# Unread products at the start of a sparse-attention and MLP kernel: eighty-eight in 64 columns for forty-four in 128, and one fewer ahead of the third local score round

## The chip, the cores and the metric

The kernel runs on one core of a Trainium2 chip. A core has five engines that run their own instruction streams side by side: TensorE (PE in the profile, with its weight loads listed as PEld), VectorE (DVE), ScalarE (ACT), GpSimd (POOL) and SyncE (SP). They wait for each other through semaphores, and transfers run on 16 DMA engines. The metric is the device time of one execution in microseconds (us); lower is better.

## The reference

Attention with fixed sparse masks on 8 batches, 8 heads, 576 positions and 64 channels, and then a two-layer MLP over the 4608 tokens (512 to 2048 to 512) with the Mish activation:

```python
scores = scale * np.matmul(q, k.transpose(0, 1, 3, 2))
mask_local = (rel >= 0) & (rel < stride)                       # heads 0 to 3
mask_strided = (rel >= 0) & (pos[None, :] % stride == pos[:, None] % stride)   # heads 4 to 7
attn = softmax(where(mask, scores, -1e9));  x = attn @ v
h = x @ w_in
g = h * np.tanh(sp)          # sp = log(1 + exp(h))
out = g @ w_out
```

`stride` is 32. The inputs and the output are float32; the kernel multiplies in bfloat16.

## The kernel before

The work is cut into 9 MLP blocks of 512 tokens (`NBLK`), and the attention of the next batch is woven in between the products of the current block. Only the places that the masks leave are computed: the local heads in windows of 96 queries against 128 keys, the strided heads in tiles of 72 positions.

The order of each engine's instructions is the order in which the code writes them (`tc.manual_schedule()`): nothing reorders it. What is told here is the beginning, batch 0, which has no MLP to hide behind; it stands in the main body from line 636 on:

- Loads are issued on three queues. `k` for the strided heads goes first on SP and ACT (L645), everything else on POOL: rest of `k` (L646), `q` and `v` of the strided heads (L110), local `k` and `q` (L123), local `v` (L137), the MLP weights `w_in` in five pieces (L166), then batch 1 and `w_out`.
- VectorE clears buffers (L651 to L674), the first of them the 640 columns of `kTs[1]` that the unread products multiply, and casts the first `k` tile (L675).
- TensorE then runs: the unread products (L678); transposes of strided `k` (`t_step`, L237), each copied out of PSUM by VectorE or ScalarE; the mask of each strided part added as a product with the identity (`bias`, L297); three more unread products (L682); transposes of strided `q`; bias; one unread product (L686); bias; three strided score rounds (`qk`, L324), with the exponential on ScalarE (L338); two unread products (L690); then `pv2` for strided tiles in pairs (L366, L371; normalised by VectorE at L396 and L397), in between transposes of the local `k` and `q` (`t_step_loc0`, L253), bias and scores of the local parts 0 and 1; transposes of the strided result (`xt`, L420); two unread products (L709); bias and scores of local part 2; `pv2` of the local windows; and the first MLP groups (`mlp1`, L575).

An unread product is made by `fill`: the cleared part of `kTs[1]` as weights, `w` columns of it as the moving operand, into a PSUM tile that nothing reads. `fill_acc(i, n, w)` takes the accumulator `i` for it; the next user of the same accumulator waits until these products have ended. In the stream each product is two instructions, a weight load (LDWEIGHTS) and a matmul.

The batch's local scores have ten products of 96 columns in parts 0 and 1 and four in part 2. `mlp1(0, accs)` runs its groups 0 and 1 first for the channels of the strided heads (2, 3), between the transposes of the local result, then the other channels, then groups 2 to 7. The whole of what lies between L678 and L717 feeds PE in order, so a product that waits holds up those behind it.

Of the kernel before, what the change touches and what calls it, by code (L numbers as in the profile page):

```python
# [40 lines left out]
def kernel(ctx, tc, q, k, v, moe_w_in, moe_w_out, out):  # L41
# [48 lines left out]
    def acc(i, name):  # L90

        return ps_a.tile([128, 2, 512], F32, tag=f"acc{i}", name=name)
# [451 lines left out]
    def fill(t, n, w=512):  # L544

        for _ in range(n):
            nc.tensor.matmul(
                t[:, 0:w], lhsT=kTs[1][:, 512:640], rhs=kTs[1][:, 0:w], start=True, stop=True
            )

    def fill_acc(i, n, w=512):
        fill(acc(i, "fill")[:, 0, :], n, w)
# [83 lines left out]
    with tc.manual_schedule():  # L636
# [38 lines left out]
        cast(Dv, ks[0][0:PN, 0:2, :], k32[0:PN])  # L675

        a = Attn(0)
        fill_acc(2, 44, 128)  # L678
        for hp in range(2):
            t_step(0, "k", hp, Sc if hp else Dv)  # L680
        a.bias("s", 0, 0)
# [24 lines left out]
        load_w_out(3, 4)  # L706
        a.xt("s", 0, Dv)
        a.xt("s", 1)
        fill_acc(0, 2)  # L709
        a.bias("l", 2, 0)  # L710
        a.qk([("l", 2)], 0)
        Sc.preload_act_table(AF.Mish)
# [119 lines left out]
```

## Time and profile before

| what | us |
|---|---|
| median of 5 runs (lowest, highest) | 309.44 (308.17, 310.79) |
| the profiled execution | 311.34 |
| its span, first to last instruction | 309.6 |
| PE busy (share of the span) | 301.0 (97%) |
| PE, unread products (52 matmuls), first and last start | 1.3 and 20.2 |
| first product of the MLP (L575) starts | 23.3 |
| ACT, POOL, DVE busy | 181.6, 105.4, 157.6 |

The profile is of one execution. Its page gives the busy time of each engine, the span in slices with the clock that TensorE was granted (1.00 is full speed), the DMA queues with their packets, and the chain of work that ended last. Other views list the instructions in order of time, the idle time of an engine before an instruction with what released it in brackets ("issue" is time in which the profile shows nothing that was waited for), and busy times by window. An `xN` at the end of a row counts instructions. Weight loads and products overlap, and the ends of products are modelled.

### The profile page before, as it was taken

Reading aid. Unit: us, or ns where it says so; the run is one execution under the profiler, and the core shown is the slowest. Engines: PE = TensorE matmul, PEld = TensorE weight load, DVE = VectorE, ACT = ScalarE, POOL = GpSimd, SP = SyncE. Lnnn points to the kernel's source line nnn. Section 1 sums busy time; section 2 is a strip of 40 time slices with the busy share of each in tenths; the row PEclk is TensorE's granted clock in tenths of the full one; section 3 lists DMA queues with packets and bytes.
Section 4 is the critical chain, followed back from the end, with each engine's and each line's share of the span. In section 5 each row is a group of like instructions: output and inputs, shape, how many; then the busy total and the mean of one; then the engine's idle time right before and its main releaser. Section 6 shows DMA issues by size and latency. Waiting matters only on the chain.

```text
span 309.6 us, 6027 instructions
## 1 busy us (share of the span) xinstructions
PE 301.0 (97%) x2504; PEld 160.9 (52%) x2504; DVE 157.6 (51%) x375; ACT 181.6 (59%) x193; POOL 105.4 (34%) x119
## 2 busy tenths in 40 slices
PE   8889999999999999999999999999999999999995
PEld 7555545544454445444569654545454544444444
DVE  4346156600870057569686978697869760000000
ACT  2655553577537663767766776677667836215501
POOL 8752339930570052514570089016800000000000
PEclk9959999999999999999999999999999999999999
DMA  8999999999999999999457998898430030011011
GB/s 137 166 205 198 200 174 149 138 162 257 170 161 173 194 162 198 185 210 192 55 88 146 208 178 171 167 190 143 109 103 2 8 126 4 0 68 70 0 66 70
DMA packets 97550, 41.81 MB, mean 135 GB/s; under 512 B 79604, under 2 KB 91460, under 8 KB 97524
## 3 DMA queue, kind: packets, MB, share of 16 engines
q1 hardware_dynamic: 71708, 28.84, 50.4%
q0 software_dynamic: 25504, 12.31, 33.2%
q8 instruction: 19, 0.31, 0.5%
q10 hardware_dynamic: 312, 0.28, 0.3%
q14 instruction: 7, 0.06, 0.1%
HBM read 36.82 MB, written 9.44 MB: 149 GB/s over the span
## 4 chain that ended last, share of the span: by engine, by line
PE 90%; DVE 4%; DMA 2%; issue 1%; POOL 1%; ACT 1%; ACTq 0%; POOLq 0%
PE psh L575 40%; PE pso L599 34%; PE po L366 5%; PE pso L626 4%; PE ps L324 3%; DMA lq<-in_k_dram 2%; DVE x_l L383 1%; DVE x_s L383 1%; PE trx L410 1%; PE trx L420 1%; DVE rden L382 1%; PE tr L253 1%; PE ps L297 1%; DVE Pl L346 1%; ACT Ps L338 0%
## 5 line engine op out<-in xcount | busy, mean ns | idle before, releaser
L575 PE MATMUL psh<-xT,w_in 128*128 128x512 bf16 (+3 forms) x648 | 130.6, 355 | 0.5 <-ACT Ps L338 0.3
L599 PE MATMUL pso<-w_out,gT 128*128 128x512 bf16 x512 | 121.7, 379 | 0.0
L581 ACT ACTIVATE gT<-psh 128x1024 bf16<-128x1024 f32 x72 | 72.4, 1023 | 46.1 <-PE psh L575 46.1
L575 PEld LDWEIGHTS <-w_in 128*128 128x128 bf16 x648 | 60.8, 98 | 55.1 <-issue 0.9
L599 PEld LDWEIGHTS <-gT 128*128 128x128 bf16 x512 | 45.5, 98 | 46.1
L445 DVE STREAM_TRANSPOSE xs_t<-x_s 32x512 bf16<-32x512 bf16 x48 | 33.7, 702 | 0.9
L606 ACT COPY osb<-pso 128x1024 f32<-128x1024 f32 x16 | 17.6, 1102 | 24.8 <-PE pso L599 14.4
L181 POOL CAST kl<-kl 96x768 bf16<-96x768 f32 x10 | 8.8, 908 | 66.8 <-DMA kl<-in_k_dram 66.8
L382 DVE RECIPROCAL rden<-po 72x4 f32<-72x4 f32 (+1 forms) x98 | 17.3, 177 | 28.0 <-PE po L366 27.8
L346 DVE TENSOR_TENSOR Ps<-Ps,consts_sb 72x864 bf16<-72x864 bf16 (+3 forms) x12 | 8.7, 721 | 39.1 <-ACT Ps L338 39.0
L436 DVE STREAM_TRANSPOSE xT<-x_l 32x384 bf16<-32x384 bf16 x48 | 27.3, 569 | 0.7
L181 DVE COPY osb<-pso 128x512 f32<-128x512 f32 (+1 forms) x2 | 1.1, 558 | 51.3 <-PE pso L626 51.3
L383 DVE TENSOR_TENSOR x_s<-po,rden 72x256 bf16<-72x256 f32 x56 | 23.6, 421 | 1.9
L338 ACT ACTIVATE Ps<-ps 72x864 bf16<-72x864 f32 (+3 forms) x21 | 17.4, 860 | 11.3 <-PE ps L324 11.3
L366 PEld LDWEIGHTS <-Ps 72*128 72x128 bf16 x256 | 15.9, 98 | 12.2 <-DVE Ps L346 1.3
L452 ACT COPY xT<-xs_t 128x576 bf16<-128x576 bf16 x8 | 21.4, 2941 | 0.0
L338 ACT ACTIVATE Pl<-ps 128x960 bf16<-128x960 f32 (+1 forms) x20 | 17.3, 876 | 6.2 <-PE ps L324 6.2
L366 PE MATMUL po<-vs,Ps 72*128 72x65 bf16 (+1 forms) x256 | 18.5, 194 | 0.4 <-DVE Ps L346 0.2
L181 POOL CAST vl<-vl 128x768 bf16<-128x768 f32 (+2 forms) x20 | 16.6, 828 | 5.7 <-DMA vl<-in_v_dram 4.4
L383 DVE TENSOR_TENSOR x_l<-po,rden 96x256 bf16<-96x256 f32 x42 | 17.7, 421 | 1.4
L179 ACT COPY xT<-trx 128x576 bf16<-128x576 bf16 x15 | 9.6, 639 | 13.6 <-PE trx L420 9.6
L346 POOL TENSOR_TENSOR Ps<-Ps,consts_sb 72x1008 bf16<-72x1008 bf16 (+1 forms) x9 | 14.5, 1637 | 6.6 <-DVE x_l L383 6.5
(93 smaller groups left out, 245.0 us busy)
## 6 DMA issues: line engine op xcount, KB each, us to landing
out_dram<-osb SPq DMA_DIRECT2D x16, 512.0 KB, 4.8
kl<-in_k_dram SPq DMA_DIRECT2D x5, 576.0 KB, 7.9
ql<-in_q_dram SPq DMA_DIRECT2D x5, 576.0 KB, 10.9
vs<-in_v_dram SPq DMA_DIRECT2D x5, 576.0 KB
vl<-in_v_dram SPq DMA_DIRECT2D x5, 576.0 KB, 10.0
w_out<-in_moe_w_out_dram POOLq DMA_DIRECT2D x4, 512.0 KB, 16.5
ks<-in_k_dram POOLq DMA_DIRECT2D x7, 288.0 KB, 9.0
qs<-in_q_dram POOLq DMA_DIRECT2D x7, 288.0 KB, 9.4
```

Source lines behind the costliest of these rows:

```text
L181: eng.tensor_copy(out_, in_)
L338: nc.scalar.activation(pt[0:n, :, 0:nw], t[0:n, :, o0:o0 + nw], AF.Exp, scale=scale)
L346: meng.tensor_tensor(out=pm, in0=pm, in1=mk[0:n, :].unsqueeze(1).unsqueeze(1).to_broadcast([n, 2, nu, w]), op=ALU.mult,)
L366: nc.tensor.matmul(po[:, h, 0:rhs.shape[-1]], lhsT=pt[0:n, c0:c0 + 128], rhs=rhs, start=True, stop=True,)
L382: nc.vector.reciprocal(rden[0:m, :], po[0:m, :, D])
L383: nc.vector.tensor_tensor(out=dst.rearrange("p (h d) -> p h d", h=4), in0=po[0:m, :, 0:D], in1=rden[0:m, :].unsqueeze(2).to_broadcast([m, ...
L436: nc.vector.transpose(dst[32 * q:32 * q + 32, :, :, m:m + 32], src[m:m + 32, :, :, q, :])
L445: nc.vector.transpose(xs_t[32 * q:32 * q + 32, :, :, m:m + 32], src[m:m + 32, :, :, q, :])
L452: nc.scalar.copy(xT[:, 2 + c, t0:t0 + S].rearrange("p (n j) -> p j n", j=CS), xs_t[:, :, c, 0:PN])
L575: nc.tensor.matmul(ps[:, u, o:o + n], lhsT=w_in[:, cc, fc * 128:(fc + 1) * 128], rhs=xT[:, cc, a:a + n], start=(cc == 2 and o == 0), stop= ...
L581: nc.scalar.activation(gT[:, 2 * g:2 * g + 2, :], ps[:], AF.Mish)
L599: nc.tensor.matmul(p[:, ot % 2, :], lhsT=gT[:, fc, 128 * ot:128 * ot + 128], rhs=w_out[:, fc, :], start=(fc == 0), stop=(fc == 15),)
```

## The change

In line 678 the forty-four unread products of 128 columns become eighty-eight of 64 columns, in the same accumulator and at the same place. In line 709, ahead of the bias and the scores of local part 2, two unread products of 512 columns become one.

```diff
         a = Attn(0)
-        fill_acc(2, 44, 128)
+        fill_acc(2, 88, 64)
         for hp in range(2):
             t_step(0, "k", hp, Sc if hp else Dv)
...
         a.xt("s", 0, Dv)
         a.xt("s", 1)
-        fill_acc(0, 2)
+        fill_acc(0, 1)
         a.bias("l", 2, 0)
         a.qk([("l", 2)], 0)
```

## The prediction

> **What bounds the kernel now.** I read the page first: TensorE (PE) is busy 97% of the 309.6 us span and the chain that ended last lies on it for 90%. So time taken out of PE's stream at the front moves everything behind it, as long as no transfer becomes the limit. Second, the timeline of PE from 9 to 24 us, the stretch that both edits bear on. Its rows give start, length, engine, line, operation and, in brackets, idle time before:
>
> ```profile
> 1.27 4.83 PE L547 MATMUL fill<-kTs 128*128 128x128 bf16 x44 [1.27 <-DVE kTs L651]
> ...
> 14.66 0.26 PE L324 MATMUL ps<-qTl,kTl 64*128 64x96 bf16 x4
> ...
> 16.41 0.42 PE L324 MATMUL ps<-qTl,kTl 64*128 64x96 bf16 x6 [1.49 <-issue]
> ...
> 19.78 1.05 PE L547 MATMUL fill<-kTs 128*128 128x512 bf16 x2
> 20.88 0.48 PE L297 MATMUL ps<-consts_sb 128*128 128x192 bf16 x2
> ...
> 23.30 1.02 PE L575 MATMUL psh<-xT,w_in 128*128 128x512 bf16 x4 [0.23 <-DVE rden L396]
> ```
>
> The first local score round has ten equal products. Four run, PE stops, six follow at 16.41. All ten read operands that the fourth already had; the releaser is "issue", so nothing that the profile shows was awaited. Third, windows over this place (busy us and count of each engine, then granted clock, DMA share, GB/s):
>
> ```profile
> 0.00:14.92 14.92, 12.92 (x222) 10.20 (x223) 5.66 (x25) 7.04 (x10) 11.72 (x20) 1.00 1.21 150
> 12.75:16.16 3.41, 1.91 (x46) 1.44 (x47) 1.78 (x4) 1.58 (x3) 2.72 (x4) 1.00 1.86 166
> 16.16:19.57 3.41, 3.16 (x47) 2.09 (x47) 1.55 (x5) 1.60 (x2) 2.50 (x4) 0.50 1.28 205
> 19.57:22.99 3.42, 3.36 (x39) 2.08 (x36) 1.45 (x3) 2.28 (x4) 0.69 (x1) 0.50 1.25 208
> 23.00:40.00 17.00, 16.77 (x125) 9.19 (x124) 7.11 (x13) 10.41 (x12) 5.87 (x8) 1.00 1.32 198
> ```
>
> The stretch that holds the stop has PE busy for 1.91 of 3.41 us; after it the granted clock is 0.50 for 6.8 us. So the stop costs twice: itself, and half speed behind it. Fourth, the DMA queues: of the whole span, and of 13.5 to 15.2 and 19.9 to 20.9 us (packets, MB, share):
>
> ```profile
> q8 instruction: 19, 0.31, 0.5%
> ...
> q8 instruction: 1, 0.02, 5.9%
> ...
> q8 instruction: 1, 0.02, 5.6%
> ```
>
> Queue q8 brings PE's code: 0.31 MB in 19 packets is 16.3 KB each, for 2504 products and as many weight loads, 264 instructions a packet. One packet moves between 13.5 and 15.2 us, and PE goes on after it. I read the stop as PE having run out of code.
>
> **Where the stop lies in the program.** Before it stand 222 products, 223 weight loads and five waits or branches that the profile doesn't count: 450 instructions. With 256 to a block (16,384 bytes at 64 each), a block begins at 450, the one before at 194. Number 194 lies in the strided score rounds, which begin at 9.44 us after a wait. From entering block 194 to running at 450 is 16.41 - 9.45 = 6.9 us. I take it that entering a block asks for the next one: the second packet, seen from 19.9 us, comes 3.5 us after PE entered block 450 at 16.4, and the first, from 13.5 us, 4.1 after 9.45. A block that PE gets through in under some 6.9 us makes it wait. Block 194 has 256 small instructions; PE did them in 5.3 us (9.45 to 14.72) and waited 1.7.
>
> The Trainium skill speaks against this: "Runtime: NRT & Kernel Launch", section "Instruction fetch mechanics", has blocks of 256 instructions too, but room for 2048 on PE and a boundary cost that is mostly hidden. By it PE would not starve at number 450, the change would save only its one removed product, 0.2 to 0.4 us, and the time would be 309.1. The 19 packets stand against the room (with 2048 held some 12 would do), and the 1.49 us idle row against "hidden". I go by the trace.
>
> **First edit: 88 products of 64 columns for 44 of 128.** *Duration.* They run before the clock is up: 44 in 4.69 us (4.83 with the last one's tail, less about 0.14) is 106.7 ns each, 128 columns at 0.83 ns. At 64 columns that is 53.3 ns, and 88 x 53.3 = 4.69 us: nothing changes. The bound from below is nothing, as the columns are the same. From above: the same skill's "TensorE: Matmul & The Clock Gate", on the gap of 56 ns, has some 62 ns per product where the sequencer decodes in software, so 88 x 62 = 5.46 us, 0.77 late. The row that is nearest denies it: in the same half-speed clock, 16 products of 64 and 1 columns with 16 weight loads start within 0.62 us (16.77 to 17.39), 39 ns each. I take 0; 0.8 is kept for the range. The cover is thin: the first q transposes wait for their load until 7.79, an idle of 0.15 us.
>
> *Position.* Eighty-eight more instructions before everything else. The block at 194 now begins at what was 106, the last of the first eight k transposes, which PE passes at 6.17 us at the latest. Adding 6.9 makes the next block ready by 13.1. That block begins at what was 362, the third pair of the local q transposes. These wait for their load until 12.93, so it is wanted at 12.97: **what is left of the stop is 0.0 to 0.15 us.** The 1.69 us (14.72 to 16.41) go. The next boundary, at 706, was 620 (86 on, since the second edit takes two away): the fourth product of the MLP's first group. Asked for at 13.0, ready at 19.9; wanted, below, at 20.2. Blocks after that take far longer than 6.9 us (the last row above: 249 instructions in 17 us).
>
> **Clock.** Without the stop, the stretch from 12.75 us loses nearly 1.5 us of idle; what waits remain (0.3 for the bias round, 0.3 for the transposes) are like those of 9.33 to 12.75, after which the clock stayed at 1.00. So I carry on at full speed from 14.72. The score round ends at 14.9; 32 products of pv2("s", 6) at 27 ns (10.80, 10.84, 10.87 in the timeline) end at 15.4. VectorE ends the pair before at 15.70 and needs 0.20 + 0.04 + 0.69, so x_s is whole at 16.65. Meanwhile bias and scores of the second local round run from 15.75 to 16.4. Sixteen transposes at 33 ns go from 16.7 to 17.25.
>
> **Second edit: one filler product fewer.** Now two take 19.78 to 20.83, and the bias round behind them waits for their end (20.88). At full speed one product is 0.22 us less on PE; at half speed 0.41. The remaining one ends at 17.65, bias and scores at 18.1 to 18.2, and the first eight of pv2("l", 0) at 18.5. VectorE is free since 18.1 (transpose copy of 0.76 us from 17.3), divides from 18.55 to 19.48, and the MLP's first group starts 0.15 later: 19.6, where it was 23.30. **The sum is -3.7 us:** 1.7 stop, 0.2 filler, 1.8 clock.
>
> **What could hide it.** Transfers now have 3.7 us less time. The five pieces of w_in are issued from 10.2 to 14.0 and take up to 12.4: the last is there at 26.4, and its first reader starts at 30.5 instead of 34.2. The first w_out piece lands at 16.65 + 16.5 = 33.1, wanted at 35.0 (38.66 - 3.7); the k and q pieces of batch 1 (15.66 + 14.8 = 30.5) at 32 to 34; its v piece (17.41 + 17.2 = 34.6) at 35.7. All hold, the closest by 1.1 us. No queue is moved past: neither edit issues a DMA, and POOL's issues wait for other transfers. Later PE is full, so the 3.7 us arrive at the end.
>
> **To the runs.** The profiled execution took 311.34 us for a span of 309.6, the median of the runs is 309.44, from 308.17 to 310.79. On its own scale the change makes 311.34 - 3.7 = 307.6. The five runs may pay the half clock in different measure: the gain in full off the slowest gives 307.1, stop and filler alone (1.9) off the fastest 306.3. Between them: **306.7 us**, 0.9% faster.
>
> **Rivals.** (1) The stop goes but half speed comes anyway, since idle shares near this place are enough for it, or the fillers run 0.8 us longer and the block comes late by as much: 309.44 - 1.7 = 307.7, up to 308.8. For it: the threshold isn't known, 1.91 of 3.41 busy was too little and 3.16 was enough. (2) The change doesn't do what it says, PE's code having nothing to do with the idle time: 309.2. Against it: the stop amid ten equal products. (3) Slower: the code packet moves at 13.5 us because the DMA engines are loaded (share 1.86), not because PE asked at 9.45. Then it is there at 16.4 as before, but PE needs it at 12.97: a stop of 3.4 us, and 1.9 us of products still to do behind it, in part at half clock: 309.44 + 1.7 + 0.9 = 312. It decides from the point at which the code comes later than 14.7. Against it: the second packet came 3.5 us after its block was entered, under the same load.
>
> **Numbers.** Forecast 0.66, rival 1 0.17, rival 2 0.07, rival 3 0.10. The forecast's own range is 305.4 to 307.9; with rival 1 the range is 305.4 to 308.9, which leaves out rivals 2 and 3. A measurement of this kernel tells 0.5% (1.5 us) from no change: below 307.9 lie the forecast and half of rival 1, 0.75; within, its other half and most of rival 2, 0.14; above 311.0 0.11.
>
> **What would show it.** Right: no idle row above 0.3 us inside the first local round, clock 1.00 from 6 to the end, first L575 product at 19.6, a q8 packet at about 10 us. The step on duration: 88 fillers from 1.27 to 5.96. Wrong: an idle row at the local q transposes near 13 us that lasts to 16.4 (rival 3), a 0.50 stretch with no stop ahead of it (rival 1), or the stop again after four of the ten products (rival 2).

## The result and the profile after

The changed kernel takes 307.63 us in the median of 44 executions (306.42 to 312.78), the kernel before 310.79 in the median of 79 (307.22 to 316.57). The ratio is 0.9915, with a 95% interval of 0.9897 to 0.9933; like all ratios below it leaves out executions more than 1.5% above the fastest of their kernel, here all 11 of the changed kernel's in which PE had half clock and only 13 of the 79 of before, while the means over all executions, 308.45 and 310.48, differ by 0.65%. The profiled execution took 307.29 us, with a span of 305.5 (before 311.34 and 309.6).

Rows of TensorE from the timeline of the changed kernel:

```profile
1.27 4.35 PE L547 MATMUL fill<-kTs 128*128 128x64 bf16 x88 [1.27 <-DVE kTs L651]
...
13.47 0.70 PE L253 MATMUL tr<-consts_sb,lq 96*64 96x96 bf16 x24 [0.54 <-DMA lq<-in_q_dram]
...
15.03 0.50 PE L324 MATMUL ps<-qTl,kTl 64*128 64x96 bf16 x10
...
17.48 0.38 PE L547 MATMUL fill<-kTs 128*128 128x512 bf16 x1
17.92 0.32 PE L297 MATMUL ps<-consts_sb 128*128 128x192 bf16 x2
...
19.91 1.02 PE L575 MATMUL psh<-xT,w_in 128*128 128x512 bf16 x4 [0.47 <-DVE rden L396]
```

The ten products of the first local score round now stand in one row: the stop between the fourth and the fifth is gone. The only longer idle rows ahead of them wait for loads. The MLP starts at 19.91 instead of 23.30, 3.4 us earlier; the other 0.7 of the 4.1 us of span come behind that point. The same stretches as in the windows of before (busy us and count by engine, granted clock, DMA share, GB/s):

```profile
12.75:16.16 3.41, 2.81 (x77) 2.19 (x74) 1.81 (x5) 2.39 (x5) 2.24 (x4) 1.00 2.05 159
16.16:19.57 3.41, 3.23 (x59) 2.05 (x59) 2.96 (x7) 2.87 (x5) 3.01 (x4) 1.00 1.28 200
19.57:22.99 3.42, 3.08 (x27) 2.00 (x28) 3.09 (x6) 1.98 (x3) 0.70 (x1) 1.00 1.24 206
```

PE is busy for 2.81 us where it was for 1.91, and the clock stays at 1.00. The code queue, over the span and from 8.3 to 9.5 us:

```profile
q8 instruction: 20, 0.33, 0.5%
...
q8 instruction: 1, 0.02, 4.9%
```

There is one packet more for 86 instructions more, and the first one moves near 8.5 us, where it was after 13.5.

Both kernels come in executions that differ by how long PE had half clock. The mean clock of an execution falls into steps: 1.00, 0.994, 0.989, 0.983, 0.978, which are 0 to 4 stretches of 3.41 us at half clock (3.41 x 0.5 / 308 = 0.0055; half clock lasted 6.8 us, two stretches, in the windows of before). Sorted so, with 147 executions of the kernel before that ran beside the experiments and 64 of the changed one:

| stretches at half clock | before: executions, median us | changed: executions, median us |
|---|---|---|
| none | 26, 308.05 | 52, 307.27 |
| 1 | 40, 310.16 | 0 |
| 2 | 74, 311.31 | 0 |
| 3 or 4 | 7, 312.8 | 12, 311.5 |

Among executions at full clock the change is worth 0.8 us; before, those with one or two stretches of half clock took 2.1 or 3.3 us more than those with none. Before, 121 of 147 executions had half clock; after, 12 of 64 (11 of the first 44, 1 of 20 later). Weighted, the change saves 310.5 - 308.1 = 2.4 us: by these classes a third at full clock (stop and filler) and two thirds from fewer executions with half clock. The split is not a clean one: half speed for 3.41 us can lose 1.7 us of products at most, so the 2.1 hold something else too, perhaps a longer stop.

### The profile page after: what moved, and what is told of

Its sections match the earlier page's. It is cut to its first block, busy times and chain, and to the rows that moved or that the text cites. A ratio compares the mean times of both kernels' runs of the same rounds, so it can differ in the third digit from the quotient of the medians.

```text
span 305.5 us, 6113 instructions
## 1 busy us (share of the span) xinstructions
PE 297.6 (97%) x2547; PEld 159.0 (52%) x2547; DVE 155.8 (51%) x375; ACT 181.6 (59%) x193; POOL 105.7 (35%) x119
## 4 chain that ended last, share of the span: by engine, by line
PE 89%; DVE 3%; DMA 3%; issue 1%; POOL 1%; ACT 1%; ACTq 0%; POOLq 0%
PE psh L575 41%; PE pso L599 33%; PE pso L626 5%; PE po L366 5%; PE ps L324 3%; DMA lq<-in_q_dram 3%; DVE x_l L383 1%; PE trx L410 1%; ACT Ps L338 1%; DVE x_s L383 1%; PE tr L253 1%; DVE rden L382 1%; PE trx L420 1%; PE ps L297 0%; POOL qs L110 0%
## 5 line engine op out<-in xcount | busy, mean ns | idle before, releaser
L346 DVE TENSOR_TENSOR Ps<-Ps,consts_sb 72x864 bf16<-72x864 bf16 (+3 forms) x12 | 7.4, 626 | 39.8 <-ACT Ps L338 39.8
L181 POOL CAST vl<-vl 128x768 bf16<-128x768 f32 (+2 forms) x20 | 15.5, 775 | 5.9 <-DMA vl<-in_v_dram 5.0
```

Source lines behind the costliest of these rows:

```text
L181: eng.tensor_copy(out_, in_)
L346: meng.tensor_tensor(out=pm, in0=pm, in1=mk[0:n, :].unsqueeze(1).unsqueeze(1).to_broadcast([n, 2, nu, w]), op=ALU.mult,)
```

## The experiments

My theory: the number of PE's instructions decides where a code block of 256 begins, PE runs dry where the block comes late, and the idle time brings half clock. Rivals: the shorter unread products themselves, the second edit, the score round, or chance in the clock. All kernels compute the full result.

**Each edit alone.**

```diff
-        fill_acc(2, 44, 128)
+        fill_acc(2, 88, 64)
```

> First edit alone (two unread products stay ahead of the third local score round). Theory of the code blocks: the 88 more instructions put the block boundary at the local q transposes near 13 us, so no idle row inside the first local score round, clock 1.00 behind it, and nearly the whole gain of the changed kernel: 0.2 us short of it, median 307.8. Rival, that the shorter unread products or the second edit make the gain: the idle row stays after four of ten products and the time stays at that of the kernel before.

Ratio 0.9902 (0.9876 to 0.9928), median 307.42, none of six executions with half clock.

```profile
1.27 4.87 PE L547 MATMUL fill<-kTs 128*128 128x64 bf16 x88 [1.27 <-DVE kTs L651]
...
15.21 0.39 PE L324 MATMUL ps<-qTl,kTl 64*128 64x96 bf16 x10
...
17.67 0.60 PE L547 MATMUL fill<-kTs 128*128 128x512 bf16 x2
```

The first edit carries the whole gain. The row of fillers also settles their price: (5.95 - 1.27) / 88 = 53.2 ns each until the next PE row at 5.95.

```diff
-        fill_acc(0, 2)
+        fill_acc(0, 1)
```

> Second edit alone (44 products of 128 columns stay). Theory of the code blocks: all instructions up to the first local score round keep their numbers, so the idle row of 1.5 us after four of ten products stays; PE gains one unread product, 0.2 us at full clock to 0.4 us at half: within 0.5% of the kernel before. Rival, that the second edit carries the gain: 2 us or more faster.

Ratio 1.0009 (0.9981 to 1.0037), median 311.04.

```profile
15.25 0.26 PE L324 MATMUL ps<-qTl,kTl 64*128 64x96 bf16 x4
16.50 0.30 PE L324 MATMUL ps<-qTl,kTl 64*128 64x96 bf16 x6 [0.99 <-issue]
...
0.00:16.00 16.00, 12.49 (x222) 9.60 (x223) 6.15 (x26) 7.00 (x10) 12.12 (x21) 1.00 1.19 149
```

The stop stands where it stood, behind 222 products and 223 weight loads as before (the last row, a window that ends in the stop), and the second edit by itself can't be measured.

**Number against shape.** If the number counts, one whole block more must bring the stop back.

```diff
-        fill_acc(2, 44, 128)
+        fill_acc(2, 172, 32)
```

> 172 products of 32 columns in place of 44 of 128, two unread products kept: 128 more products are 256 more instructions, one whole block, and the fillers should still end at about 5.9 us at half clock (172 x 27 ns = 4.6 us). Theory of the code blocks: the boundary falls on the same product of the first local score round again, so the stop comes back there, about 1.5 us after four of ten products, and the time is that of the kernel before within 0.5%. Rival, that more and shorter fillers are what helps: no stop, as fast as with 88.

Ratio 0.9992 (0.9966 to 1.0018), median 311.07.

```profile
1.27 4.74 PE L547 MATMUL fill<-kTs 128*128 128x32 bf16 x172 [1.27 <-DVE kTs L651]
...
15.25 0.26 PE L324 MATMUL ps<-qTl,kTl 64*128 64x96 bf16 x4
15.79 0.30 PE L324 MATMUL ps<-qTl,kTl 64*128 64x96 bf16 x6 [0.28 <-issue]
...
0.00:15.70 15.70, 12.90 (x350) 10.27 (x351) 5.83 (x26) 7.00 (x10) 12.75 (x22) 1.00 1.25 160
```

With still more and shorter products the stop is back after four of ten, to the instruction, behind 350 products and 351 weight loads (222 + 128, 223 + 128), and so is the time. That rules out the shape of the fillers and fits a period of 256. The stop is only 0.28 us in this execution and the clock stayed at 1.00 behind it, as in five of the 22; the other 17 had half clock, and none of them was profiled. Here block and packet can be followed: the block before was entered in the strided scores at 10.19 and the code ran at 15.79, 5.6 us, against 6.9 in the profile of before.

**Fewer instructions.**

```diff
-        fill_acc(2, 44, 128)
+        fill_acc(2, 22, 256)
```

> 22 products of 256 columns in place of 44 of 128, two unread products kept: 44 instructions fewer. Theory of the code blocks: the boundary moves 44 instructions on, to the bias products of the second local round (L297); the block before it is entered at about 9.5 to 9.9 us, so its code is there at 16.4 to 16.8: all ten products of the first local round run together, and the stop is ahead of or between the two bias products, some 0.7 to 1.1 us (of which 0.3 is a wait for VectorE anyway). Time 0.5 to 1 us under the kernel before. Rival, that the place of the stop has to do with the score round itself: it stays after four of ten.

Ratio 0.9949 (0.9924 to 0.9973), median 309.23; 12 of 22 executions without half clock.

```profile
14.81 0.50 PE L324 MATMUL ps<-qTl,kTl 64*128 64x96 bf16 x10
...
15.90 0.28 PEld L297 LDWEIGHTS <-consts_sb 128*128 128x128 bf16 x2 [0.16 <-DVE x_s L397]
...
16.08 0.56 PE L297 MATMUL ps<-consts_sb 128*128 128x480 bf16 x2 [0.25 <-PE po L371]
```

The ten run together, so the round has nothing to do with it. The boundary lies at the bias products, and the idle time there is 0.25 us. VectorE releases their weight load at 15.90; the first product starts at 16.08, where in the changed kernel load and product start together (16.12). So the code costs some 0.2 us and was there at 16.1, earlier than I said; the gain, 1.4 us by the medians, is more than the 0.5 to 1 that I gave. Moving the boundary under another wait hides most of the stop.

**Half the shift, and one and a half blocks.**

```diff
-        fill_acc(2, 44, 128)
+        fill_acc(2, 66, 85)
```

> 66 products of 85 columns in place of 44 of 128, two unread products kept: half of the shift of the changed kernel. Theory of the code blocks: the boundary falls on the bias product (L297) ahead of the first local score round, wanted at about 14; the block before it is entered in the q transposes at 7.9, and from entering to running it took 5.6 us (172 products) to 6.9 us (before), so the code is there at 13.5 to 14.8: an idle row of 0 to 0.7 us at L297 and no longer one after four of ten. Median between the changed kernel and the one before, 307.4 to 309. Rival, that only the full 88 clear it: as before, 310.6.

Ratio 1.0014 (0.9984 to 1.0045), median 311.71.

```profile
12.74 0.98 PE L253 MATMUL tr<-consts_sb,lq 96*64 96x96 bf16 x24
14.21 0.57 PE L297 MATMUL ps<-consts_sb 128*128 128x480 bf16 x2 [0.49 <-PE tr L253]
15.13 0.39 PE L324 MATMUL ps<-qTl,kTl 64*128 64x96 bf16 x10
...
0.00:14.00 14.00, 11.98 (x222) 9.74 (x223) 5.73 (x24) 6.60 (x10) 10.82 (x19) 1.00 1.20 155
```

The place was right: idle time now stands at L297, 0.49 us, again behind 222 products and 223 weight loads, and the round is whole. (The releaser named is PE's own product before it, which ended at 13.72; nothing else that the profile shows was awaited.) The time was not: I had 307.4 to 309. Eleven of 22 executions had three or four stretches of half clock and only three had none. The profiled one is the only one with a single stretch, so how long the stop is in the others is not known; the boundary at this place cost as much as at the old one.

```diff
-        fill_acc(2, 44, 128)
+        fill_acc(2, 132, 43)
```

> 132 products of 43 columns in place of 44 of 128, two unread products kept: twice the shift. Theory of the code blocks: the first boundary does no harm (it falls on the first strided products at about 11, its block having been entered among the fillers), but the next one, 256 further, falls on the transposes of the strided result (L420), wanted at about 17.1; its block was entered at about 11 and is there at 16.6 to 17.9: an idle row of 0 to 0.8 us in or ahead of L420, and half clock in part of the runs. Median 307.5 to 310. Rival, that more and shorter unread products help without bound: as the changed kernel, 307.4, with no idle row at L420.

Ratio 0.9946 (0.9907 to 0.9985), median 308.56, seven of ten executions without half clock. The profile taken is of one with three stretches, and it has no idle row at L420, so it doesn't show the second stop that I expected; the theory is not confirmed here. Nor can this execution speak against it: at half clock PE came to L420 at 19.38, when the code packet, landed at 15.6, had long been there. The seven at full clock have a median of 308.40, 1.1 us above the changed kernel's 307.27; the filler that this kernel keeps is some 0.2 of it by the prediction's sum, and the rest is not explained. The profile shows something else. Waits of PE in its first 26 us, and two windows of the same execution:

```profile
PE tr L237 <- DMA qs<-in_q_dram: 0.9, 1, 0.9
PE tr L253 <- DMA lq<-in_k_dram: 0.5, 1, 0.5
PE tr L253 <- DMA lq<-in_q_dram: 0.4, 1, 0.4
...
10.80:14.26 3.46, 2.51 (x68) 1.76 (x64) 1.28 (x4) 3.17 (x5) 2.25 (x3) 1.00 1.91 176
14.26:24.50 10.24, 9.95 (x130) 6.49 (x131) 5.33 (x13) 5.53 (x7) 6.21 (x9) 0.50 1.37 193
```

Waits for loads, without a stop, were followed by 10.2 us of half clock.

**Idle time with the code in place.** On the changed kernel:

```diff
+        for _ in range(3):
+            cast(Sc, kTs[1][:, 0:640], kTs[1][:, 0:640])
         a.qk([("l", 0)], 1)
+        fill(tile_t("fill"), 1)
         a.pv2("s", 6, 0)
```

> The changed kernel with an idle PE put back where the stop was, with its code in place: three copies of 640 columns on ScalarE ahead of the first local score round, and one unread product behind the round that waits for them (1.5 us of idle PE; all ten products of the round run together). Theory that the idle time itself brings the half clock: 0.50 for 3.4 to 6.8 us from about 16 us in most runs, and a median of 309.5 to 311.5, as before the change. Rival, that half clock goes with the missing code and not with idle time, or that it is chance: clock 1.00 as in the changed kernel, and at most 1.5 us are lost, median under 309.

Ratio 1.0057 (1.0033 to 1.0081), median 312.31. Timeline, and windows of the same execution:

```profile
14.84 0.39 PE L324 MATMUL ps<-qTl,kTl 64*128 64x96 bf16 x10
...
16.82 0.39 PE L547 MATMUL fill<-kTs 128*128 128x512 bf16 x1 [1.60 <-ACT kTs L179]
...
14.30:17.70 3.40, 1.80 (x45) 1.38 (x44) 0.89 (x3) 3.27 (x5) 3.15 (x5) 0.98 1.43 194
17.60:24.40 6.80, 6.51 (x65) 3.63 (x62) 4.72 (x11) 3.42 (x5) 2.15 (x4) 0.50 1.24 205
```

A wait of the stop's length, just behind the stop's place, with the code long there (its packet moved at 8.1 us), brings 6.8 us of half clock, and all 22 executions had some (the changed kernel: 12 of 64). So idle time brings it, and no missing code is needed. The median came out 0.8 us above what I gave.

**What remains of half clock.** On the changed kernel, in both cases with fewer fillers at the front, so that later instructions keep their numbers:

```diff
-        fill_acc(2, 88, 64)
+        fill_acc(2, 86, 64)
...
-        fill_acc(2, 3)
+        fill_acc(2, 5)
```

> The changed kernel with five instead of three unread products of 512 columns ahead of the q transposes, where PE waits up to 0.7 us for a load, and 86 instead of 88 products at the beginning, so that all later instructions keep their numbers. About a quarter of the executions of the changed kernel have half clock for some 10 us. Theory that idle time in the first 10 us brings it: fewer of these, the median of the others within 0.3 us of 307.4. Rival, that it comes from elsewhere (where the clock's stretches begin): the same share, and up to 0.4 us lost where the load comes early.

Ratio 0.9892 (0.9853 to 0.993), median 307.62; one of six executions with half clock. Too few to tell the share; no loss.

```diff
-        fill_acc(2, 88, 64)
+        fill_acc(2, 85, 64)
...
         a.pv2("s", 0, 0)
+        fill(tile_t("fill"), 1)
...
         a.pv2("s", 2, 1)
+        fill(tile_t("fill"), 2)
```

> The changed kernel with one unread product of 512 columns ahead of the local k transposes and two ahead of the local q transposes, where PE waits 0.2 and 0.5 us for loads, and 85 instead of 88 at the beginning, so that all later instructions keep their numbers. Theory that what is left of half clock in the changed kernel comes from idle PE before 14 us: fewer executions with half clock than in the changed kernel run beside it, the others within 0.4 us of it, median the same or lower. Rival, that it comes from elsewhere: the same share, and up to 0.6 us lost where the loads come early.

Ratio 0.9937 (0.991 to 0.9964), median 307.81; 4 of 23 with half clock.

> The changed kernel once more, beside the one before it in this list, for the share of executions with half clock: about a quarter (11 of 44 at first), median 307.4 to 307.7.

Ratio 0.9913 (0.9891 to 0.9936), median 307.01; 1 of 20 with half clock. Beside it the extra fillers lose 0.8 us (307.73 against 306.95 among executions at full clock) and don't visibly lower the share; both numbers are small. No version beat the changed kernel clearly. The profile of the extra fillers is of an execution of 314.71 us, with three stretches of half clock, and shows one way into them:

```profile
13.21 0.23 PE L253 MATMUL tr<-consts_sb,lq 96*64 96x96 bf16 x2 [0.16 <-ACT kTl L179]
15.13 0.66 PE L253 MATMUL tr<-consts_sb,lq 96*64 96x96 bf16 x22 [1.68 <-issue]
```

PE stops for 1.68 us after the second local q transpose, where the prediction put the boundary of the changed kernel. The code packet moved only at 12.2 us, and PE went on 2 us after it had landed. Again 223 weight loads stand before the stop.

## Why the prediction was right, point by point

- **Total.** Forecast 306.7 us, 0.9% faster; measured 307.63 and 0.85% (0.67 to 1.03). The forecast is 0.9 us low, under even the 307.27 of the executions at full clock, and it stood on five executions of before with a median of 309.44, where 79 have 310.79: that both percentages agree so well is in part luck. In the profiled pair the first MLP product comes 3.4 us earlier for a forecast of 3.7; the span is shorter by 4.1, and the 0.7 us behind that product were put at nothing and are not explained.
- **The stop is missing code.** Held. It follows the number of instructions: away with +88, back at the same product with +256, at the bias round with +44 and -44.
- **Duration of the fillers.** 53.3 ns forecast, 53.2 measured with the first edit alone. In the changed kernel's profile the clock rose before they ended (they start 53 ns apart up to 4.9 us and 29 ns apart from there), so the next row comes at 5.54 instead of 5.96. The dearer figure of 62 ns was not seen.
- **Where the block begins, and what is left of the stop.** The place held. The 0.0 to 0.15 us held in the profile of the changed kernel, whose load came 0.54 us later than before and whose packet had landed by 9.4, but not always: 6.9 us from entering a block to running the next was one sample, taken as a constant. In the profiles it was 5.6 us (172 products) and about 9 (extra fillers: entered before 6.2, run at 15.13). That 12 executions in 64 of the changed kernel still have half clock may come from the stop at the q transposes or from waits for loads; both were seen to lead into it, each in another kernel, and how often each does in this one was not measured.
- **Stop 1.7, clock 1.8, filler 0.2.** The split fits the profiled execution of before, which had a long stop and two stretches of half clock. Over all executions it is 0.8 for stop and filler together and some 1.7 for the clock, as far as the classes above can part them. The stop was the term that was too large: executions that kept full clock lost only 0.8 to stop and filler. That these are the ones with a short stop, as in the profile with 172 products, is argued, not shown.
- **Filler ahead of the third round.** 0.2 us forecast; alone it moved nothing that can be measured, and the first edit is as fast without it.
- **Transfers.** The 1.1 us of margin were enough: no load shows as a wait of the MLP in the profile after.
- **Rivals.** Half clock all the same (rival 1) happens in 12 of 64 executions, mostly for 10 us; none of them was profiled, so whether a stop goes ahead of it there is open, but 132 products show half clock with none. PE's code having nothing to do with it (rival 2) fell with 172 products. That the code moves at a time set by the load alone (rival 3) fell in the changed kernel, with a packet at 8.5 us; but a packet at 12.2 with the extra fillers, and a stop of 1.68 us, show that it can be late all the same; whether the load has a part in that was not tested.

## What to carry to other kernels

An idle row with the releaser "issue" in the midst of equal small products is worth a count of instructions: if code packets of 256 move near it, adding or taking away instructions far ahead shifts the boundary to a place where the engine waits anyway or has long products queued. Judge such a change by where every later boundary falls and not by the one that it mends. Idle time of PE costs more than itself where it also brings half clock, so look at the granted clock behind each wait, over many executions and not one, and add up the idle time of all waits in a stretch of some 3.4 us rather than weigh each by itself.

## What the hardware did that I had not expected

- Half clock came in whole stretches of 3.41 us, one to four of them, and the median time rises with their number: 308.05, 310.16, 311.31 us for none, one, two. Single executions overlap (one stretch took 308.73 to 312.2).
- The stretches have a fixed grid within an execution. In the six profiled executions that had half clock at the start, it began 10.24 us (five of them) or 13.65 us after full clock had begun, three or four times 3.41, and full clock had begun anywhere from 3.99 to 7.31 us. The stretch just ahead of half clock had PE busy for 1.57 us (extra fillers), 1.82 (idle put back), 1.91 (before), 2.43 (second edit alone), 2.47 (132 products) and 2.64 (66 products). Full clock also followed stretches of 2.41 (132 products, from 7.40), 2.43 and 2.35 us (172 products, from 5.65 and 84.16). So between 2.35 and 2.65 both were seen, and behind less than that only half clock, the end of the execution apart. It is the idle time in one stretch together that goes with it, and where the grid lies decides which waits fall together. That this makes executions of one kernel differ would fit, but was not tested. The stretch ahead and the one at half clock, with 66 products:

```profile
13.03:16.44 3.41, 2.64 (x65) 1.96 (x59) 1.71 (x5) 2.25 (x4) 2.58 (x4) 1.00 1.72 179
16.44:19.85 3.41, 3.35 (x32) 1.72 (x30) 2.15 (x4) 1.70 (x3) 2.46 (x4) 0.50 1.26 207
```

- Code was run 1.2 to 2.1 us after its packet had landed (before 15.13 and 16.41; with 22 products 14.84 and 16.08; with extra fillers 13.08 and 15.13), and the packet itself moved 1.5 to 6 us after the block before was entered (about 6.4 and 7.8 with the first edit alone, 6.2 and 12.2 with extra fillers). What makes that time so different is open.
- Over its executions, the kernel with a stop of 0.49 us at 13.7 in its profile (66 products) had at least as much half clock as the one with 1.49 at 14.9: 18 of 22 executions with two stretches or more, against 81 of 147.
